# First x by token steps of both streams, the diagonal of reciprocals in two operations, and a first weight slice of 256 columns

## The chip, the cores and the metric

The kernel runs on one core of one Trainium2 chip. The metric is the device time of one execution in microseconds, as the median of several runs. A core has a tensor engine (PE in the profile, its weight loads PEld), a vector engine (DVE), a scalar engine (ACT), GpSimd (POOL), and SyncE (SP), which here issues DMAs only. Each engine works through its own instructions in order and waits for the others by semaphores. DMAs are issued from SP (queue q1, hardware_dynamic) and from GpSimd (queue q0, software_dynamic) and are carried out by 16 DMA engines.

## The reference

A short causal convolution along the sequence, whose taps are a softmax over the kernel positions of each head, and behind it a feed-forward block with a rectified gate:

```python
w = np.exp(weight - weight.max(-1, keepdims=True))
w = w / (w.sum(-1, keepdims=True) + 1e-9)              # [H=8, K=7]
x_pad = zeros(6 rows) + x                               # x: [B=8, S=4096, D=192]
out[b, s, h, g] = sum_k w[h, k] * x_pad[b, s + k, h, g] # head h has 24 of the 192 channels
y = out.reshape(32768, 192)
result = (np.maximum(y @ w_gate, 0) * (y @ w_val)) @ w_out   # 192 -> 1536 -> 192
```

Inputs and output are float32.

## The kernel before, in words

**Streams and units.** The eight sequences are handled as two streams of four (`st` 0 and 1, `NB` = 4 sequences apart). A unit is 1024 tokens of both streams, a window 512 tokens; there are 16 units. A tile of activations holds channel group c (64 of the 192 channels, three groups) of stream 0 on partitions 0 to 63 and of stream 1 on partitions 64 to 127. The gate and value weights (`Wg`, `Wv`) stand on both halves of the partitions, so that the two streams are multiplied side by side.

**Main part.** For each unit, `gate_val` (L528) goes over 12 slices f of 128 hidden columns: 12 matmuls of 512 columns (two weights, three channel groups, two streams), in pairs; ACT takes the gate through a ReLU into `gr` (L552), DVE multiplies it with the value into `hT` (L553). The results stand in PSUM tiles of two banks; the pool `ps` has four buffers that are given out in turn, so f+2 needs the buffers of f. `project` (L636) multiplies `hT` with `Wo` (L570), and ACT and DVE move the result out. For most tokens the convolution is done by ACT, DVE and GpSimd on transposed tiles (the lanes), beside PE's matmuls.

**The start.** For the first windows the convolution runs on PE, as matmuls of x (tokens on partitions) with banded matrices that hold the taps of one head on their diagonals. This is where the change lies. In order of the code:

- SP loads `weight` (L101), then x. The first window of 512 tokens is cut into five token steps `jj`: step 0 has 96 tokens, steps 1 to 4 have 104 each, with 6 rows of the step before. SP brings steps 1 to 4 of stream 0 in float32 into a staging area (`stage`, in the tile `prods`, L122), and step 0 of both streams (L138), whose padding DVE clears first (L137). GpSimd brings steps 1 to 4 of stream 1 with a cast to 16 bits straight into the tile `x_h` (L127).
- GpSimd clears `spaced` (L126), and selects ones on its diagonals (L128); from it DVE makes `same` and `places` by reductions (L238), patterns of ones that spread a coefficient over a band.
- The weights come by columns, in slices `CUTS = [0, 128, 384, 640, 896, 1152, 1536]`, by GpSimd's queue (`load_w`, L167 to L173), onto partitions 0 to 63; a copy (`both_halves`, L175 to L177) brings them to the other half: DVE does slices 0 and 1, GpSimd the later ones. GpSimd issues slices 0 to 2, then the x of the second window (`load_x`, L86), then slices 3 to 5 with copies between.
- Coefficients: DVE the negated maximum (L251), ACT the exponentials into `ex` (L254), DVE their sum and its reciprocal `sm` (L258, L259) and `over` = identity times the reciprocal (L261); PE spreads `over` over the exponentials (L272), DVE makes `diag` (L282), PE makes the bands in PSUM (L292, 14 matmuls). ACT makes `taps` (L304), which SP copies to all partitions in ten small DMAs (L310). `fill_band` moves the bands to SBUF: heads 0 to 3 by DVE, heads 4 to 7 by ACT (L329). The bands of heads 0 to 3 and 4 to 7 stand in two different PSUM tiles, `bps` and `spread`.
- ACT casts the staged steps 1 to 4 of stream 0 (L317), in two parts by channels; DVE casts step 0 (L335).
- `warm_up` (L152 to L155) puts dummy matmuls of ones into the waits of PE: seven ahead of the coefficients (six of 512 columns and one of 256), and one of 512 after each of the two steps that make the bands.
- `first_block` (L387) does the 120 convolution matmuls of the first window (L377), group by group; for group 0 stream 0 comes before stream 1. Each group has its own PSUM tile, and is moved to `xc` by ACT, DVE and ACT (L392). At the start of group 0 DVE copies weight slice 0 to the other half. After the block DVE copies slice 1 (L661), and `gate_val` begins. `second_block` (L394), the same for the next window, stands within the sixth f of the first `gate_val`.

## Time and profile before

| what | value |
|---|---|
| median of 3 runs | 765.98 us (765.98 to 766.01) |
| span of the profiled execution | 764.4 us |
| PE busy | 760.3 us (99%) |
| DVE busy | 705.6 us (92%) |
| ACT busy | 600.9 us (79%) |
| first matmul of the first `gate_val` | at 7.66 us |

The span runs from the first to the last instruction of the profiled execution; the time of a run holds about 1.6 us more than that. In the profile a line of a timeline gives start and length in us, engine, line of the code, operation, output <- inputs, shapes, and in square brackets how long the engine had been idle before and what ended that. A line of the stages gives a stretch of time, then its length, then the busy time of PE, PEld, DVE, ACT and POOL with the number of instructions, the granted clock, the share of the DMA engines and GB/s. A line of the chain gives start, length and what carried the chain in that time. A line of a DMA queue gives packets, MB, and the share of the 16 engines' time.

### The profile page before, as it was taken

To read this page: it belongs to the slowest core of one execution; us is meant where nothing else is said; L and a number is where in the kernel's file an instruction comes from. 1 tells how busy PE (TensorE), PEld (TensorE's weight loads), DVE (VectorE), ACT (ScalarE), POOL (GpSimd) and SP (SyncE) were. 2 spreads that over 40 slices of the span, in tenths; PEclk is the share of its full clock that TensorE was granted. 3 is DMA by queue.
4 is the path that set the end of the run, shared out by engine and by line. 5 is a ranking of instruction groups with operands and counts; after the bars stand their busy time and mean duration, and the time that the engine had idled before them with its cause. 6 is when DMAs were issued, how large, how long until landed. Compare 5 with 4: busy or idle time off the path is not lost.

```text
span 764.4 us, 25103 instructions
## 1 busy us (share of the span) xinstructions
PE 760.3 (99%) x10929; PEld 501.3 (66%) x10929; DVE 705.6 (92%) x763; ACT 600.9 (79%) x735; POOL 378.4 (50%) x244
## 2 busy tenths in 40 slices
PE   9999999999999999999999999999999999999998
PEld 5494674947649476584855848567494674947648
DVE  7998999999999999999999999999999999999891
ACT  6787887878878887887878878787787887876571
POOL 9419448093571926729175390853909347090000
PEclk9999999999999999999999999999999999999999
DMA  9969039290452805528073271722819134220202
GB/s 123 134 102 148 7 96 81 65 111 22 95 67 83 97 23 107 49 85 94 30 112 40 85 94 44 120 16 90 89 44 125 13 97 60 66 48 15 71 1 84
DMA packets 131830, 56.00 MB, mean 73 GB/s; under 512 B 96392, under 2 KB 131720, under 8 KB 131720
## 3 DMA queue, kind: packets, MB, share of 16 engines
q1 hardware_dynamic: 90680, 38.81, 23.9%
q0 software_dynamic: 40896, 15.50, 20.3%
q8 instruction: 85, 1.39, 0.8%
q14 instruction: 25, 0.20, 0.1%
q10 hardware_dynamic: 144, 0.10, 0.0%
HBM read 31.48 MB, written 25.17 MB: 74 GB/s over the span
## 4 chain that ended last, share of the span: by engine, by line
PE 99%; DVE 0%; ACT 0%; issue 0%
PE ps L541 65%; PE ps L570 32%; PE ps L619 1%; PE ps L377 0%; PE ps L154 0%; PE ps L411 0%; DVE band L329 0%; PE ps L272 0%; ACT acc L596 0%; PE ps L292 0%
## 5 line engine op out<-in xcount | busy, mean ns | idle before, releaser
L553 DVE TENSOR_TENSOR hT<-gr,ps 128x1024 f16<-128x1024 f16 (+1 forms) x386 | 469.0, 1216 | 36.6 <-ACT gr L552 9.4
L552 ACT ACTIVATE gr<-ps 128x1024 f16<-128x1024 f32 (+1 forms) x386 | 392.9, 1019 | 101.9 <-PE ps L541 99.7
L491 POOL TENSOR_TENSOR prods<-prods 128x1344 f32<-128x1344 f32 x70 | 212.4, 3034 | 290.0 <-DVE prods L487 286.7
L541 PE MATMUL ps<-xc,Wg 64*128 64x512 f16 x2304 | 311.9, 376 | 0.0
L541 PE MATMUL ps<-xc,Wv 64*128 64x512 f16 x2304 | 311.9, 376 | 0.0
L570 PEld LDWEIGHTS <-hT 64*128 64x128 f16 x5952 | 245.9, 94 | 3.7
L570 PE MATMUL ps<-Wo,hT 64*128 64x192 f16 x5952 | 248.1, 243 | 0.0
L541 PEld LDWEIGHTS <-Wv 64*128 64x128 f16 x2304 | 129.8, 94 | 118.5 <-DVE hT L553 0.3
L541 PEld LDWEIGHTS <-Wg 64*128 64x128 f16 x2304 | 112.3, 94 | 132.8 <-issue 0.2
L515 DVE SCALAR_TENSOR_TENSOR acc<-x_r,tap,acc 128x576 f32<-128x576 f16 x225 | 165.3, 813 | 0.0
L485 ACT ACTIVATE prods<-x_r,tap 128x448 f32<-128x448 f16 x222 | 130.1, 660 | 0.0
L596 ACT COPY out_s<-ps 128x768 f32<-128x768 f32 (+1 forms) x64 | 45.5, 711 | 51.3 <-PE ps L570 40.0
L203 POOL DMA_DIRECT2D x_e<-in_x_dram x58 | 47.0, 823 | 16.6 <-ACT acc L501 12.8
L465 POOL COPY x_p<-x_e 128x960 f16<-128x960 f16 (+1 forms) x58 | 50.3, 906 | 1.2 <-DMA x_e<-in_x_dram 1.1
L491 POOL TENSOR_TENSOR xc<-prods 128x1344 f16<-128x1344 f32 x14 | 42.4, 3029 | 1.1
L515 DVE SCALAR_TENSOR_TENSOR xc<-x_r,tap,acc 128x576 f16<-128x576 f16 x45 | 34.1, 813 | 0.0
L501 ACT ACTIVATE acc<-x_r,tap 128x576 f32<-128x576 f16 x45 | 31.4, 763 | 0.0
L487 DVE TENSOR_SCALAR prods<-x_r,tap 128x448 f32<-128x448 f16 x70 | 26.6, 450 | 0.0
L596 DVE COPY out_s<-ps 128x384 f32<-128x384 f32 (+1 forms) x16 | 8.7, 541 | 11.9 <-PE ps L619 9.4
L619 PE MATMUL ps<-Wo,hT 128*128 128x192 f16 x96 | 8.1, 246 | 0.0
L619 PEld LDWEIGHTS <-hT 128*128 128x128 f16 x96 | 7.9, 98 | 0.2 <-issue 0.2
L154 PE MATMUL ps<-const-bfloat16-1.0 128*128 128x512 bf16 (+1 forms) x9 | 3.9, 572 | 0.8 <-PEq L719 0.8
(54 smaller groups left out, 56.3 us busy)
## 6 DMA issues: line engine op xcount, KB each, us to landing
out_dram<-out_s SPq DMA_DIRECT2D x62, 384.0 KB, 2.7
x_e<-in_x_dram POOLq DMA_DIRECT2D x34, 192.0 KB, 7.4
x_e<-in_x_dram POOLq DMA_DIRECT2D x24, 240.0 KB, 5.6
x_r<-x_p SPq DMA_TRANSPOSE x131, 5.1
Wo<-in_moe_w_out_dram POOLq DMA_DIRECT2D x1, 576.0 KB, 7.3
x_h<-in_x_dram POOLq DMA_DIRECT2D x2, 210.0 KB, 4.8
Wg<-in_moe_w_gate_dram POOLq DMA_DIRECT2D x4, 96.0 KB, 4.1
Wv<-in_moe_w_val_dram POOLq DMA_DIRECT2D x4, 96.0 KB, 4.0
```

Source lines behind the costliest of these rows:

```text
L203: first = nc.gpsimd.dma_start(out=xe[:, j0 + start : j0 + n, st, :, :].rearrange("p j c r -> p j (c r)"), in_=bass.AP(tensor=x.tensor, off ...
L465: nc.gpsimd.tensor_copy(out=xp[:, j0 : j0 + n, :, st, :], in_=xe[:, j0 : j0 + n, st, :, :])
L485: engine.activation(out=out, in_=in_, func=ACTF.Copy, scale=scale)
L487: engine.tensor_scalar(out=out, in0=in_, scalar1=scale, scalar2=None, op0=ALU.mult)
L491: nc.gpsimd.tensor_tensor(out=pr[:, 0] if k < KW - 1 else xc[v + 1][:, :, LDVE:UNIT], in0=pr[:, 0], in1=pr[:, k], op=ALU.add,)
L501: nc.scalar.activation(out=accs[v][:, c, :], in_=shifted(v, c, 0, 0), func=ACTF.Copy, scale=tap[:, c, 0:1],)
L515: nc.vector.scalar_tensor_tensor(out=xc[v][:, c, 0:LDVE] if k == KW - 1 else acc[:, c, :], in0=shifted(v, c, k, 0), scalar=tap[:, c, k : k ...
L541: nc.tensor.matmul(out=pss[i][:, st, :], lhsT=W[64 * st : 64 * st + 64, c, 128 * f : 128 * (f + 1)], rhs=xcb[64 * st : 64 * st + 64, c, WI ...
L552: nc.scalar.activation(out=gr[:, sts], in_=pss[0][:, sts], func=ACTF.Relu)
L553: nc.vector.tensor_tensor(out=h[:, f, sts], in0=gr[:, sts], in1=pss[1][:, sts], op=ALU.mult)
L570: mm = nc.tensor.matmul(out=outs[q], lhsT=h[64 * r : 64 * r + 64, f, st, 128 * q : 128 * (q + 1)], rhs=Wo[64 * r : 64 * r + 64, f, :], sta ...
L596: one(out=dst[:, step * j : step * j + step], in_=src[:, step * j : step * j + step])
```

## The change

- **x by token steps.** SP brings step 1 and step 2 of both streams in a DMA each, then step 0, all staged in float32. GpSimd brings steps 3 and 4, one DMA for each stream. ACT casts steps 1 and 2 (one operation each, both streams), DVE step 0, which now comes after both of DVE's bands.
- **GpSimd's order.** It no longer clears `spaced` (DVE does), and its first work is the DMA of `Wg`'s slice 0, then the selection, then its two x DMAs, then `Wv`'s slice 0, then the rest as before.
- **Slices.** `CUTS` becomes six slices of 256 columns. DVE copies the first 128 columns of slice 0 to the other half before the first block and the other 128 after it, then slice 1.
- **Diagonal.** `ex` has a ninth row: 2 to the 127th off the diagonal and 0 on it, made by DVE from `spaced` ahead of the maximum. `over` is then the sum over all nine rows and its reciprocal: two operations; off the diagonal that is as good as zero. `same` is made between maximum and sum. The sum and reciprocal for the taps are made later, behind `diag`, and the product with them moves from ACT to DVE.
- **Order of the first block.** Group 0 steps 1 and 2, group 1 steps 1 and 2, group 0 step 0, group 0 steps 3 and 4 in another PSUM tile, then the rest of group 1, then group 2. Group 0 is moved to `xc` by ACT in two parts. All four PSUM buffers are taken.
- **Dummies.** One of 512 columns less at the start, and the last one has 256 columns instead of 512.

```diff
--- before.py
+++ after.py
@@ -112,19 +112,38 @@
 
     xts[0] = xpool.tile([128, GSUB, 2, D], F16, name="x_h")
 
-    def body(st):
-        return bass.AP(
-            tensor=x.tensor,
-            offset=x.offset + (NB * st * S + FIRST - PAD) * D,
-            ap=[[D, SUB], [DSUB * D, GSUB - 1], [1, D]],
+    BYSP = 3
+
+    def first_x(jj, rows, tok):
+        nc.sync.dma_start(
+            out=stage(PAD if jj == 0 else 0, rows, 0, 2, jj, 1),
+            in_=bass.AP(
+                tensor=x.tensor,
+                offset=x.offset + tok * D,
+                ap=[[D, rows], [NB * S * D, 2], [1, D]],
+            ),
         )
 
-    nc.sync.dma_start(out=stage(0, SUB, 0, 1, 1, GSUB - 1), in_=body(0))
+    Wg = const.tile([128, NCH, DFF], F16)
+    Wv = const.tile([128, NCH, DFF], F16)
+    Wo = const.tile([128, NFF, D], F16)
+    CUTS = [0, 256, 512, 768, 1024, 1280, DFF]
+
+    def load_w(s, which=3):
+        cols = slice(CUTS[s], CUTS[s + 1])
+        for src, dst in ((moe_w_gate, Wg), (moe_w_val, Wv))[which == 2 : 1 + (which > 1)]:
+            nc.gpsimd.dma_start(
+                out=dst[0:64, :, cols],
+                in_=src.rearrange("(c p) f -> p c f", p=64)[:, :, cols],
+            )
+
+    for jj in range(1, BYSP):
+        first_x(jj, SUB, FIRST - PAD + DSUB * (jj - 1))
     ones = const.tile([128, SUB], FP)
     nc.vector.memset(ones[:], 1.0)
     spaced = const.tile([SUB, KW, SEG + 2 * GAP], FP)
-    nc.gpsimd.memset(spaced[:], 0.0)
-    nc.gpsimd.dma_start(out=xts[0][0:SUB, 1:GSUB, 1, :], in_=body(1))
+    nc.vector.memset(spaced[:], 0.0)
+    load_w(0, 1)
     nc.gpsimd.affine_select(
         out=spaced[:, :, GAP : GAP + SEG],
         in_=ones[0:SUB, 0 : KW * SEG].rearrange("p (k s) -> p k s", k=KW),
@@ -134,13 +153,18 @@
         base=0,
         channel_multiplier=1,
     )
+    for st in range(2):
+        nc.gpsimd.dma_start(
+            out=xts[0][0:SUB, BYSP:GSUB, st, :],
+            in_=bass.AP(
+                tensor=x.tensor,
+                offset=x.offset + (NB * st * S + FIRST - PAD + DSUB * (BYSP - 1)) * D,
+                ap=[[D, SUB], [DSUB * D, GSUB - BYSP], [1, D]],
+            ),
+        )
+    load_w(0, 2)
     nc.vector.memset(stage(0, 32, 0, 2, 0, 1), 0.0)
-    nc.sync.dma_start(
-        out=stage(PAD, FIRST, 0, 2, 0, 1),
-        in_=bass.AP(
-            tensor=x.tensor, offset=x.offset, ap=[[D, FIRST], [NB * S * D, 2], [1, D]]
-        ),
-    )
+    first_x(0, FIRST, 0)
     spare = const.tile([H, 1], FP)
     nc.scalar.activation(spare[:], ones[0:H, 0:1], ACTF.Exp)
 
@@ -155,25 +179,13 @@
                 out=warm[:, n % 2, 0:w], lhsT=busy[:, 0:128], rhs=busy[:, 0:w], start=True, stop=True
             )
 
-    warm_up(512, 512, 512, 512, 512, 512, 256)
-
-
-
-    Wg = const.tile([128, NCH, DFF], F16)
-    Wv = const.tile([128, NCH, DFF], F16)
-    Wo = const.tile([128, NFF, D], F16)
-    CUTS = [0, 128, 384, 640, 896, 1152, DFF]
-
-    def load_w(s, which=3):
-        cols = slice(CUTS[s], CUTS[s + 1])
-        for src, dst in ((moe_w_gate, Wg), (moe_w_val, Wv))[which == 2 : 1 + (which > 1)]:
-            nc.gpsimd.dma_start(
-                out=dst[0:64, :, cols],
-                in_=src.rearrange("(c p) f -> p c f", p=64)[:, :, cols],
-            )
-
-    def both_halves(copy, s, dst):
-        cols = slice(CUTS[s], CUTS[s + 1])
+    warm_up(512, 512, 512, 512, 512, 256)
+
+
+
+    def both_halves(copy, s, dst, half=None):
+        lo, hi = CUTS[s], CUTS[s + 1]
+        cols = slice(lo, hi) if half is None else slice(lo + 128 * half, lo + 128 * half + 128)
         copy(out=dst[64:128, :, cols], in_=dst[0:64, :, cols])
 
     def pool_halves(s):
@@ -218,7 +230,10 @@
                     )
                 yield
 
-    load_w(0)
+    def cast_first(copy, jj):
+        rows = FIRST + PAD if jj == 0 else ROWS0
+        copy(out=xts[0][0:rows, jj, :, :], in_=stage(0, rows, 0, 2, jj, 1))
+
     load_w(1)
     load_w(2)
     load_rest(load_x(1))
@@ -229,8 +244,17 @@
     pool_halves(3)
     load_w(5, 2)
 
-    ex = const.tile([H, KW + 1, SEG], FP)
+    ex = const.tile([H, KW + 2, SEG], FP)
     nc.vector.memset(ex[:], 1e-9)
+    FAR = 2.0**127
+    nc.vector.tensor_scalar(
+        out=ex[:, KW + 1, 0:H],
+        in0=spaced[0:H, 0, GAP : GAP + H],
+        scalar1=-FAR,
+        scalar2=FAR,
+        op0=ALU.mult,
+        op1=ALU.add,
+    )
     some = spaced[:, 0, 0:1]
 
     def summed(out, step, n, at):
@@ -251,22 +275,19 @@
     nc.vector.tensor_reduce(
         out=mx[:], in_=wr[:], axis=mybir.AxisListType.X, op=ALU.max, negate=True
     )
+    same = const.tile([SUB, SEG], FP)
+    summed(same[:], pitch_k, SEG, GAP)
     nc.scalar.activation(
         ex[:, 0:KW, :], wr[:].unsqueeze(2).to_broadcast([H, KW, SEG]), ACTF.Exp, bias=mx[:]
     )
-    sm = const.tile([H, 1], FP)
-    nc.vector.tensor_reduce(out=sm[:], in_=ex[:, :, 0], axis=mybir.AxisListType.X, op=ALU.add)
-    nc.vector.reciprocal(sm[:], sm[:])
     over = const.tile([H, H], FP)
-    nc.vector.tensor_scalar(
+    nc.vector.tensor_reduce(
         out=over[:],
-        in0=spaced[0:H, 0, GAP : GAP + H],
-        scalar1=sm[:],
-        scalar2=None,
-        op0=ALU.mult,
+        in_=ex[:, :, 0:H].rearrange("h k j -> h j k"),
+        axis=mybir.AxisListType.X,
+        op=ALU.add,
     )
-    same = const.tile([SUB, SEG], FP)
-    summed(same[:], pitch_k, SEG, GAP)
+    nc.vector.reciprocal(over[:], over[:])
     summed(places[:, SUB - SEG : SUB - SEG + SEG + KW - 1], pitch_k - 1, SEG + KW - 1, GAP)
     spread = psum.tile([128, 2, 512], FP, name="ps")
     nc.tensor.matmul(
@@ -298,10 +319,17 @@
                 skip_group_check=True,
             )
 
-    warm_up(512)
+    warm_up(256)
 
     taps = const.tile([H, KW], FP)
-    nc.scalar.activation(taps[:], ex[:, 0:KW, 0], ACTF.Copy, scale=sm[:])
+    sm = const.tile([H, 1], FP)
+    nc.vector.tensor_reduce(
+        out=sm[:], in_=ex[:, 0 : KW + 1, 0], axis=mybir.AxisListType.X, op=ALU.add
+    )
+    nc.vector.reciprocal(sm[:], sm[:])
+    nc.vector.tensor_scalar(
+        out=taps[:], in0=ex[:, 0:KW, 0], scalar1=sm[:], scalar2=None, op0=ALU.mult
+    )
     tap = const.tile([128, NCH, KW], FP)
     for h in range(H):
         r = G * h
@@ -313,11 +341,8 @@
             )
             r += n
 
-    for cols in (slice(0, 64), slice(64, D)):
-        nc.scalar.copy(
-            out=xts[0][0:ROWS0, 1:GSUB, 0, cols],
-            in_=stage(0, ROWS0, 0, 1, 1, GSUB - 1)[:, :, cols],
-        )
+    cast_first(nc.scalar.copy, 1)
+    cast_first(nc.scalar.copy, 2)
     bands = {}
 
     def fill_band(a, heads, copy):
@@ -332,10 +357,10 @@
         )
 
     fill_band(0, [0, 1, 2], nc.vector.tensor_copy)
-    nc.vector.tensor_copy(
-        out=xts[0][0 : FIRST + PAD, 0, :, :], in_=stage(0, FIRST + PAD, 0, 2, 0, 1)
-    )
     fill_band(0, [3], nc.vector.tensor_copy)
+    cast_first(nc.vector.tensor_copy, 0)
+    both_halves(nc.vector.tensor_copy, 0, Wg, 0)
+    both_halves(nc.vector.tensor_copy, 0, Wv, 0)
     fill_band(1, [4, 5], nc.scalar.copy)
     fill_band(1, [6, 7], nc.scalar.copy)
 
@@ -349,26 +374,18 @@
     PLACE = {0: (0, 0, 0), 1: (0, 0, 1), 3: (0, 1, 0), 4: (0, 1, 1)}
     PLACE |= {6: (1, 0, 0), 7: (1, 0, 1), 2: (1, 1, 0), 5: (1, 1, 1)}
 
-    def conv_dense(g, c, ps, bank):
+    def conv_dense(g, c, ps, bank, steps):
 
 
         xt = xts[g]
-        if g == 0 and c == 0:
-            xc[0] = xcpool.tile([128, NCH, UNIT], F16, name="xc")
-            both_halves(nc.vector.tensor_copy, 0, Wg)
-            both_halves(nc.vector.tensor_copy, 0, Wv)
         toks = GROUPS[g][1]
         t0 = toks[0]
         ends = toks[1:] + [t0 + WIN]
-        late = (1, 2, 3, 4, 0)
-        both = [(jj, (0, 1)) for jj in late]
-        if g == 0 and c == 0:
-            both = [(jj, (st,)) for st in range(2) for jj in late[0:4]] + both[4:]
-        for jj, sts in both:
+        for jj in steps:
             col, n = toks[jj] - t0, ends[jj] - toks[jj]
             rows = n + PAD
             for second in range(2):
-                for st in sts:
+                for st in range(2):
                     for k2 in range(2):
                         k = 2 * c + k2
                         h0, h1 = 32 * k // G, (32 * k + 31) // G
@@ -385,18 +402,27 @@
                         )
 
     def first_block():
-        for c in range(NCH):
-            ps = psum.tile([128, 2, 512], FP, name="ps")
-            conv_dense(0, c, ps, 0)
-            copy = nc.vector.tensor_copy if c == 1 else nc.scalar.copy
-            copy(out=xc[0][:, c, 0:WIN], in_=ps[:, 0, :])
+        xc[0] = xcpool.tile([128, NCH, UNIT], F16, name="xc")
+        early, late, *rest = [psum.tile([128, 2, 512], FP, name="ps") for _ in range(4)]
+        cut = GROUPS[0][1][BYSP]
+        held, by_pool = (1, 2), range(BYSP, GSUB)
+        conv_dense(0, 0, early, 0, held)
+        conv_dense(0, 1, rest[0], 0, held)
+        conv_dense(0, 0, early, 0, (0,))
+        conv_dense(0, 0, late, 0, by_pool)
+        nc.scalar.copy(out=xc[0][:, 0, 0:cut], in_=early[:, 0, 0:cut])
+        nc.scalar.copy(out=xc[0][:, 0, cut:WIN], in_=late[:, 0, cut:WIN])
+        conv_dense(0, 1, rest[0], 0, (0, *by_pool))
+        nc.vector.tensor_copy(out=xc[0][:, 1, 0:WIN], in_=rest[0][:, 0, :])
+        conv_dense(0, 2, rest[1], 0, (1, 2, 0, *by_pool))
+        nc.scalar.copy(out=xc[0][:, 2, 0:WIN], in_=rest[1][:, 0, :])
 
     def second_block():
         two, one = [psum.tile([128, 2, 512], FP, name="ps") for _ in range(2)]
-        conv_dense(1, 0, two, 0)
-        conv_dense(1, 1, two, 1)
+        conv_dense(1, 0, two, 0, (1, 2, 3, 4, 0))
+        conv_dense(1, 1, two, 1, (1, 2, 3, 4, 0))
         nc.scalar.copy(out=xc[0][:, 0:2, WIN : 2 * WIN], in_=two[:])
-        conv_dense(1, 2, one, 0)
+        conv_dense(1, 2, one, 0, (1, 2, 3, 4, 0))
         nc.vector.tensor_copy(out=xc[0][:, 2, WIN : 2 * WIN], in_=one[:, 0, :])
 
     def conv(g):
@@ -656,6 +682,8 @@
 
 
     first_block()
+    both_halves(nc.vector.tensor_copy, 0, Wg, 1)
+    both_halves(nc.vector.tensor_copy, 0, Wv, 1)
     both_halves(nc.vector.tensor_copy, 1, Wg)
     both_halves(nc.vector.tensor_copy, 1, Wv)
     pool_halves(4)
```

## The prediction, made before the changed kernel ran

> **What bounds the kernel now.** I read the page first, then the busy time by stages, then the chain that ended last in the first 30 us, then each engine's timeline there.
>
> ```profile
> span 764.4 us, 25103 instructions
> PE 760.3 (99%) x10929; PEld 501.3 (66%) x10929; DVE 705.6 (92%) x763; ACT 600.9 (79%) x735; POOL 378.4 (50%) x244
> ```
> ```profile
> 7.65:11.00 3.35, 3.35 (x36) 1.61 (x34) 2.65 (x6) 2.59 (x5) 3.30 (x6) 1.00 1.28 134
> 11.00:24.00 13.00, 13.00 (x228) 6.66 (x228) 11.36 (x11) 10.13 (x11) 12.86 (x18) 1.00 1.10 131
> 24.00:100.00 76.00, 76.00 (x1116) 51.49 (x1114) 71.80 (x77) 62.20 (x81) 35.10 (x25) 1.00 0.58 92
> ```
>
> The second number of a stage is PE's busy time: from 7.65 us on PE has no idle time. The change touches nothing that PE does after that, so it is worth what it moves the start of PE's continuous work, plus any new stall in the first steps of it. The profiled execution has a span of 764.4 us and the runs have a median of 765.98; the 1.6 us between them lie outside the span, and I carry a difference from one to the other unchanged.
>
> ```profile
> 0.85 2.93 PE ps L154 x7
> 3.78 0.47 PE ps L272 x2
> ...
> 5.09 0.52 DVE band L329
> ...
> 5.65 2.08 PE ps L377 x106
> 7.72 6.66 PE ps L541 x60
> 14.38 1.48 PE ps L377 x120
> ```
> ```profile
> 6.18 1.38 PEld L377 LDWEIGHTS <-x_h 110*32 110x32 f16 x104 [0.15 <-DMA x_h<-in_x_dram]
> ...
> 10.96 0.33 PEld L541 LDWEIGHTS <-Wv 64*128 64x128 f16 x6 [0.34 <-DVE hT L553]
> ```
> ```profile
> 7.66 0.39 PE L541 MATMUL ps<-xc,Wg 64*128 64x512 f16 x2
> ```
>
> The start is a chain: coefficients, bands at 5.09, the first block's 120 convolution matmuls from 5.65, the gate from 7.66. In the first block 104 of the 120 had to wait, to 6.18, for the second stream of x, which GpSimd's queue brings; the second block does 120 in 1.48 us, **12.3 ns** each. The last stall is at 10.96, where f=2 waits for DVE's hT: PE is barely held there, but DVE has no more to give. These two, the gate's start and that hT, are where the sum is read.
>
> **The change, part by part.**
>
> ```profile
> 5.12 0.92 ACT L317 CAST x_h<-prods 110x256 f16<-110x256 f32 x2 [1.60 <-DMA prods<-in_x_dram]
> 5.96 0.58 ACT L329 CAST band<-ps 128x224 f16<-128x224 f32 x2
> ...
> 9.00 3.18 ACT L552 ACTIVATE gr<-ps 128x512 f16<-128x512 f32 x5 [0.48 <-PE ps L541]
> ```
>
> *x by token steps.* Before, SP's first x DMA (one stream, steps 1 to 4) has landed at 5.12. After, SP brings steps 1 and 2 of both streams, together the same bytes, then step 0. So I take step 2 as landed at 5.12 and step 1 somewhat before. ACT then has, behind step 2's landing, one cast of 384 elements instead of 768: half of 0.92, 0.46, with both pairs of bands behind it as now. Now it goes from 5.12 to 6.54, 1.42; after, 1.42 - 0.46 = 0.96, so 6.08. PE's order now puts 16 matmuls of channel group 1 (steps 1 and 2) second. They write the PSUM buffer that held half the bands, so they wait for ACT's last band: 6.08, and 6.13 with a handoff. The first 16 matmuls, of group 0, lie ahead of that. Behind the wait stand 120 - 16 = 104 matmuls, as many as stand behind 6.18 now, but now these take 7.66 - 6.18 = 1.48, because 16 of them run for one stream alone; at the second block's pace they take 104 x 12.3 ns = 1.28. The gate starts at 6.13 + 1.28 + about 0.05 = **7.46**, 0.20 earlier.
>
> GpSimd's x, steps 3 and 4, must be there by 6.13 + (16 + 8) x 0.0123 = 6.43; the same queue's x is usable at 6.18 now. That holds if the weights put ahead of it cost under 0.25 us. What decides it:
>
> ```profile
> 0.81 0.33 POOL L126 MEMSET spaced<- 112x280 f32 x1 [0.29 <-POOLq L719]
> 1.42 0.88 POOL L127 DMA_DIRECT2D x_h<-in_x_dram  x1 [0.28 <-issue]
> 2.39 0.36 POOL L128 TENSOR_SCALAR_AFFINE_SELECT spaced<-ones 112x112 f32<-112x112 f32 x1
> 2.67 0.68 POOL L170 DMA_DIRECT2D Wg<-in_moe_w_gate_dram  x1
> ```
> ```profile
> 42.22 0.85 POOL L203 DMA_DIRECT2D x_e<-in_x_dram  x1 [12.75 <-ACT acc L501]
> ```
> ```profile
> q0 software_dynamic: 12, 0.00, 4.2%
> ```
> ```profile
> q1 hardware_dynamic: 45, 0.03, 29.9%
> ```
> ```profile
> q1 hardware_dynamic: 487, 0.36, 104.1%
> ```
>
> The last three rows are the DMA queues in 42.2 to 43.9, 2.2 to 3.0 and 3.0 to 4.1 us. From 2.2 to 3.0 SP's queue (q1) is the only one at work and fills 30% of the engines; from 3.0 to 4.1 it fills them, still alone. GpSimd's x was issued by 2.30 and shows no packet before 4.1. At 42.22 an issue of 0.85, over at 43.07, has its first packets before 43.9, within 0.8 us. So either GpSimd's packets stood behind SP's, or its first issue is slow (1.8 us). After, the first issue is Wg with twice the columns, from 0.8 to 1.1 (the 0.28 of issue time may stay), over at 1.5 to 2.0. With 0.8 us it moves in the 70% that are empty from 2.3 to 3.0: 0.7 x 0.8 = 0.56 us of full engines, about what it needs (192 packets of 1 KB read are 0.2 MB, and q1 moves 0.36 MB in 1.1 us: 0.6 us). With 1.8 us it meets SP's x. I take the former, and keep the latter as rivals. Then GpSimd's x lands at 6.1 to 6.3 and Wv, as long a transfer as both slices now, at about 6.75, as now.
>
> [...]
>
> *Weights and DVE.*
>
> ```profile
> 1.07 0.38 DVE L137 MEMSET prods<- 32x384 f32 x1
> ...
> 2.79 0.15 DVE L258 TENSOR_REDUCE sm<-ex 8x1 f32<-8x8 f32 x1 [0.45 <-ACT ex L254]
> 2.98 0.15 DVE L259 RECIPROCAL sm<-sm 8x1 f32<-8x1 f32 x1
> 3.25 0.22 DVE L261 TENSOR_SCALAR over<-spaced,sm 8x8 f32<-8x8 f32 x1
> 3.39 0.35 DVE L238 TENSOR_REDUCE same<-spaced 112x16 f32<-112x112 f32 x1
> ...
> 5.09 0.51 DVE L329 CAST band<-ps 128x336 f16<-128x336 f32 x1 [0.51 <-PE ps L292]
> 5.67 0.36 DVE L335 CAST x_h<-prods 102x384 f16<-102x384 f32 x1
> ...
> 6.49 0.28 DVE L177 COPY Wg<-Wg 64x384 f16<-64x384 f16 x1 [0.27 <-DMA Wg<-in_moe_w_gate_dram]
> 6.75 0.58 DVE L177 COPY Wv<-Wv 64x384 f16<-64x384 f16 x1
> 7.36 0.69 DVE L392 CAST xc<-ps 128x512 f16<-128x512 f32 x1
> 8.08 0.42 DVE L177 COPY Wg<-Wg 64x768 f16<-64x768 f16 x1
> 8.43 0.53 DVE L177 COPY Wv<-Wv 64x768 f16<-64x768 f16 x1
> 9.62 2.48 DVE L553 TENSOR_TENSOR hT<-gr,ps 128x512 f16<-128x512 f16 x4 [0.67 <-ACT gr L552]
> ```
>
> Ahead of xc (L392) DVE has the same two copies of 384 elements, the second from 6.75. Each takes 0.28 to 0.58, so they are over at 7.03 to 7.33; group 1 is ready 0.30 ahead of the gate (7.36 against 7.66), at 7.16. xc runs from about 7.2 to 7.9. Behind it come two **added** copies (the second half of the 256 columns), 0.56 to 0.86 with their 0.28 to 0.58 each, then slice 1 as now, 8.08 to 8.96, 0.88. DVE is free at 9.35 to 9.75, middle 9.5. The first hT needs ACT's gr as well: 9.62 - 7.66 = 1.96 behind the gate, 9.42. So hT moves from 9.62 to 9.5, the added copies eating the idle 0.67 in front of it, and f=2 with it, from 10.96 to 10.84. Sum: 0.20 won at the gate, 0.08 of it lost to the copies: **-0.12**, with ends -0.2 (ACT decides) and +0.13 (both added copies slow).
>
> *Diagonal.* Now reduction, reciprocal and product go from 2.79 to 3.47, 0.68. After, one reduction over 8 x 9 elements (between 0.15 for 8 and 0.35 for 112; 0.27) and a reciprocal of 8 (0.15 from the row for one; up to 0.22), 0.45 in all, and `same` goes into the wait for the exponential. Against it, the row of large numbers (a product like the 0.22) now stands ahead of the maximum on DVE and waits for GpSimd's selection, whose end I put at 1.95 to 2.45 (the Wg issue, 0.68 to 0.88, then 0.36 and handoffs) against 2.75 now. The maximum moves by 0 to +0.5. The diagonal is ready at 3.25 to 3.75, now 3.47. Either way it is covered: the first 16 matmuls need the bands at 5.9, now 5.60, since the ACT wait stands at 6.13. I count 0, and up to +0.2 if every bound is the bad one. The reciprocal and product for the taps go to DVE between the diagonal and the bands, into the 0.51 of idle time ahead of 5.09: 0.52 there, at most 0.1 over, under the same cover. SP's ten tap DMAs start later, and are read long after this stage. The memset that moves to DVE (280 elements, under the 0.38 for 384) runs beside DMA latency; step 0's DMA waits behind it on SP, up to 0.3 later, and lands at about 5.7 to 6.0 with 0.36 of cast on DVE, wanted at 6.13 + 16 x 0.0123 = 6.33. Just covered.
>
> *Warm-up.* PE loses 768 columns of the dummy matmuls. They hide only in the wait, but the tensor clock opens through them:
>
> ```profile
> 4.18 0.61 PE L154 MATMUL ps<-const-bfloat16-1.0 128*128 128x512 bf16 x1
> ...
> 5.09 0.38 PE L154 MATMUL ps<-const-bfloat16-1.0 128*128 128x512 bf16 x1
> ```
>
> A 512-column matmul takes 0.61 at 4.18 and 0.38 at 5.09: the faster pace came between them, about 4 us behind PE's first matmul. After, the first run of dummies ends 2.93/6.5 = 0.45 earlier, and PE waits that long for the diagonal. I count 0; the other end is rival D. [...]
>
> Slices of 256 columns from the second on are wanted one f later than now; GpSimd's copies of the last shrink. Under a PE that is busy throughout, nothing.
>
> **How it adds up.** 765.98 - 0.12 = 765.86, so **765.9**.
>
> **The rivals.**
>
> A, *more is won*: the group-1 matmuls wait for the first pair of bands alone (half of 0.58 earlier) or x lands earlier. DVE then decides: -0.2 to -0.45, 765.6. For it: bands 4 and 5 are all that they read. Against: the buffer is shared with 6 and 7.
>
> B, *slower: Wg takes turns with SP's x.* Its 0.6 us of transfer stretch step 2's landing by 0.4, to 5.5. ACT, and the gate behind it, go to 7.86, xc to 8.25, hT to 9.85: +0.25, 766.2. It decides from a landing at 5.25, where the 0.12 are gone. For it: a first issue that shows packets only after 1.8 us. Against: q1 alone from 3.0 to 4.1.
>
> C, *Wg stands behind SP's x*: GpSimd's x lands 0.5 later, 6.65; behind it 80 matmuls, 1.0; gate 7.7. Wv lands at 7.25, its copy ends at 7.55 to 7.85, xc at 8.25 to 8.55, hT at 9.7 to 10.3: +0.1 to +0.65, 766.35.
>
> D, *the clock opens late*: conv at half pace (+1.48) and part of the gate: +1.2 to +2, 767.4. For it: less dummy work. Against: PE is still busy most of the time.
>
> E, *the diagonal is no earlier*: covered, the same time as the forecast; it is within it.
>
> **How the numbers follow.** Forecast 0.45, A 0.12, B 0.22, C 0.16, D 0.05. Forecast alone: 765.75 to 766.1. The range takes in A, B and C with their bounds: **765.5 to 766.6**; D is left out, and what my bounds miss at either end, together under 0.2. About 0.2%, 1.5 us, is what a measurement of this kernel can tell from no change; the whole stage that the change touches holds 7.66 us and moves by tenths. Only D reaches past it: slower 0.04, faster 0.01, within 0.95.
>
> **What would show it.** Right: Wg's packets between 2.2 and 3.0 on the software queue; ACT's second cast at about 5.1; conv's second group at about 6.1; gate at 7.45; DVE without idle time from xc to hT, hT at 9.5. Wrong: the second cast at 5.4 or later (B); conv waiting for x_h past 6.4, or xc behind a late Wv copy (C); convolution matmuls at twice 12.3 ns (D); any PE idle time behind 11 us, which I hold for excluded.

## The result, and the profile after

The change makes the kernel slower. After: 768.94 us, median of 6 runs (767.78 to 770.02); before, beside it: 765.98 us (765.92 to 766.41). The ratio is **1.0037 [1.0026, 1.0048]**, +2.96 us; forecast were 765.9 and, at most, 766.6. The runs of the kernel after spread over 2.2 us, those of before over 0.5. The profiled run after took 768.67 us. Times here are medians and ratios compare means; the kernel before has long executions of its own (13 of the 102 beside the experiments took 767.4 to 768.0), which widen every interval.

The page after, and its stages:

```profile
span 766.8 us, 25104 instructions
PE 761.8 (99%) x10928; PEld 503.6 (66%) x10928; DVE 706.4 (92%) x769; ACT 601.3 (78%) x735; POOL 378.0 (49%) x244
```
```profile
0.00:7.65 7.65, 6.04 (x86) 3.49 (x90) 4.31 (x19) 3.80 (x8) 6.43 (x14) 1.00 0.80 129
7.65:11.00 3.35, 3.35 (x82) 1.98 (x72) 2.14 (x6) 0.92 (x3) 3.31 (x6) 1.00 1.28 144
11.00:24.00 13.00, 13.00 (x228) 6.76 (x226) 10.72 (x12) 10.31 (x13) 11.88 (x16) 1.00 0.95 109
```

PE is without idle time from 7.65 us on, as before, and does the same 228 matmuls from 11 to 24 us. So the time, all but 0.4 of it, was lost ahead of 11 us, though in the second row PE is no less busy than it was (matmuls of 24.2 ns count there as busy as those of 12.3, see below). The chain that ended last, to 18 us:

```profile
1.32 0.80 POOL Wg L135
2.13 0.08 POOLq L147 x2
2.20 0.01 issue
2.22 0.36 POOL spaced L147
2.58 0.64 POOL x_h L157
3.22 3.99 DMA x_h<-in_x_dram
7.21 0.04 issue
7.25 1.89 PE ps L394 x60
9.15 7.33 PE ps L567 x53
```

Before, the chain ran through coefficients and bands; now it is GpSimd's second x DMA, third in its queue. The timeline of the same execution shows the rest:

```profile
2.61 0.16 DVE L250 TENSOR_SCALAR ex<-spaced 8x8 f32<-8x8 f32 x1 [0.58 <-POOL spaced L147]
...
3.28 0.26 DVE L284 TENSOR_REDUCE over<-ex 8x8 f32<-8x72 f32 x1 [0.18 <-ACT ex L280]
...
3.58 0.19 DVE L290 RECIPROCAL over<-over 8x8 f32<-8x8 f32 x1
...
3.91 0.51 PE L293 MATMUL ps<-over,ex 8*112 8x8 f32 x2 [0.56 <-DVE over L290]
...
5.36 0.51 ACT L235 CAST x_h<-prods 110x384 f16<-110x384 f32 x1 [1.27 <-DMA prods<-in_x_dram]
...
5.78 0.59 ACT L354 CAST band<-ps 128x224 f16<-128x224 f32 x2
...
7.25 1.89 PE L394 MATMUL ps<-band,x_h 110*32 110x104 f16 x78 [0.19 <-DMA x_h<-in_x_dram]
7.74 0.29 DVE L189 COPY Wv<-Wv 64x384 f16<-64x384 f16 x1 [1.09 <-DMA Wv<-in_moe_w_val_dram]
...
8.33 0.69 DVE L416 CAST xc<-ps 128x512 f16<-128x512 f32 x1 [0.31 <-PE ps L394]
...
9.08 0.61 PE L567 MATMUL ps<-xc,Wg 64*128 64x512 f16 x2
...
10.58 0.38 PE L567 MATMUL ps<-xc,Wg 64*128 64x512 f16 x2
...
11.01 0.81 PE L567 MATMUL ps<-xc,Wg 64*128 64x512 f16 x6
```

Three things stand in it. **x is late**: the 78 matmuls that need it start at 7.25 (before, 104 started at 6.18). **PE runs at half pace**: those 78 take 1.89, 24.2 ns each instead of 12.3, and the gate's first matmuls take 0.61, which becomes 0.38 only at 10.58. The column of the granted clock reads 1.00 throughout; the pace of equal matmuls shows it, and so does the trace's record of the clock, whose entry for the full clock begins at 10.38 here and at 4.78 before; I say that the clock opens there. **The diagonal is late**: DVE's row of large numbers waits for GpSimd's selection to 2.61, and `over` is ready at 3.77 (before 3.47), behind PE's last dummy, which ends at 3.35.

The gate starts at 9.08 instead of 7.66, +1.42: x +1.07, and 9.08 - 7.25 = 1.83 for the 78 matmuls behind it, where 104 took 1.48, +0.35. At the pace of before (1.48 / 104 = 14.2 ns) the 78 would take 1.11. The twelve matmuls of the first f, at half pace to about 10.4, take 1.93 instead of 1.34, +0.59, and f=1 stands at +2.01. So in this execution half pace holds 0.72 (1.83 - 1.11) + 0.59 = 1.31 of it, and the late x, less the 26 matmuls that no longer stand behind it, 1.07 - 0.37 = 0.70. The second block stands at +2.07, and so does ACT's last copy, before and after:

```profile
761.40 0.32 ACT acc L596
```
```profile
763.47 0.32 ACT acc L622
```

The spans end at 764.36 and 766.84, so 0.41 more is lost behind that copy. In the trace SP closes the program with a row of semaphore waits, 0.06 us each; behind the wait for the last output no further one stood before, and seven stand there now. Every kernel of this document that was built from the changed one takes 3.39 to 3.42 us from PE's last matmul to the end of the span, and every one built from the kernel before takes 2.96 to 2.99. So these 0.41 belong to the change, and the smallest part of it that was run (x by steps, below) has them already. 2.01 + 0.06 + 0.41 = 2.48 is the whole difference of the spans; another 0.2 of the profiled run's time lies outside the span.

What the DMA queues moved, before and then after (packets, MB, share of the engines), from 1.5 to 5.1 us and from 5.1 to 6.2:

```profile
q0 software_dynamic: 319, 0.12, 28.0%
q1 hardware_dynamic: 688, 0.49, 50.0%
```
```profile
q0 software_dynamic: 276, 0.12, 30.3%
q1 hardware_dynamic: 696, 0.49, 50.7%
```
```profile
q0 software_dynamic: 640, 0.19, 163.3%
```
```profile
q0 software_dynamic: 330, 0.12, 111.3%
```

By 5.1 us both kernels had moved the same bytes on each queue. But GpSimd's 0.12 MB were x before, and now most of them are `Wg` (192 packets of 512 bytes, 0.10 MB), which landed at 5.14. From 5.1 to 6.2 GpSimd's queue moved 0.12 instead of 0.19 MB. x, 0.17 MB, landed at 7.21 instead of 6.14; `Wv` at 7.72 instead of 6.73.

### The profile page after: what moved, and what is told of

It reads as the page before. It is cut to its first block, busy times and chain, and to the rows that moved or that the text cites. A ratio compares the mean times of both kernels' runs of the same rounds, so it can differ in the third digit from the quotient of the medians.

```text
span 766.8 us, 25104 instructions
## 1 busy us (share of the span) xinstructions
PE 761.8 (99%) x10928; PEld 503.6 (66%) x10928; DVE 706.4 (92%) x769; ACT 601.3 (78%) x735; POOL 378.0 (49%) x244
## 4 chain that ended last, share of the span: by engine, by line
PE 99%; DMA 1%; POOL 0%; issue 0%; ACT 0%; POOLq 0%
PE ps L567 65%; PE ps L596 32%; PE ps L645 1%; DMA x_h<-in_x_dram 1%; PE ps L394 0%; PE ps L437 0%; POOL Wg L135 0%; POOL x_h L157 0%; POOL spaced L147 0%; ACT acc L622 0%; POOLq L147 0%; POOLq L747 0%
## 5 line engine op out<-in xcount | busy, mean ns | idle before, releaser
L579 DVE TENSOR_TENSOR hT<-gr,ps 128x1024 f16<-128x1024 f16 (+1 forms) x386 | 469.1, 1216 | 37.2 <-ACT gr L578 10.4
L394 PE MATMUL ps<-band,x_h 110*32 110x104 f16 (+7 forms) x240 | 4.6, 248 | 0.2 <-DMA x_h<-in_x_dram 0.2
```

Source lines behind the costliest of these rows:

```text
L579: nc.vector.tensor_tensor(out=h[:, f, sts], in0=gr[:, sts], in1=pss[1][:, sts], op=ALU.mult)
```

## The experiments

Theory 1 is the clock: 768 dummy columns less and a later diagonal leave gaps on PE, and the clock opens later, in the two profiles at 10.38 instead of 4.78; the stretch with the open clock is then 757.76 us long instead of 761.17. This step of 3.41 us is what the expectations call a window. Its rivals are the transfers: the order of GpSimd's queue (`Wg` ahead of x) and, formed later and called theory 3, the bytes that have to come through the DMA engines by the first f, whatever their order. Each expectation spells out what it takes for granted. "Dummies of before" are 512 x 6 and 256, and 512 behind the bands; "of after" 512 x 5 and 256, and 256.

### The kernel after, with the dummies of before

```diff
-    warm_up(512, 512, 512, 512, 512, 256)
+    warm_up(512, 512, 512, 512, 512, 512, 256)
...
-    warm_up(256)
+    warm_up(512)
```

> The changed kernel with the dummy matmuls of the kernel before (seven at the start, 512 columns at the end). Theory 1, the clock: the 768 columns less let PE idle from 3.35 to 3.91 us and the clock opens at 10.4 instead of 4.8; with them it opens before the convolution, whose 78 late matmuls then take 1.0 us instead of 1.8 and the first f 1.3 instead of 1.9, so about 1.4 us come back: 767.0 to 767.6, with little spread. Theory 2, the order of the DMAs alone: GpSimd's x still lands at 7.2, PE waits for it anyway, and the time stays 768 to 770 with a late clock.

768.19 us (767.3 to 770.06), 1.0025 [1.0015, 1.0035]. The median is 0.75 lower than that of the change, less than the spread of either (767.78 to 770.02 there), and short of the 767.0 to 767.6 expected. In its profile the clock still opened at 10.21; the dummies did not bring it forward in this execution. x landed at 7.59, with unchanged DMAs: in the four profiles with this order it landed between 6.89 and 7.59.

### The kernel before, with the dummies of after

```diff
-    warm_up(512, 512, 512, 512, 512, 512, 256)
+    warm_up(512, 512, 512, 512, 512, 256)
...
-    warm_up(512)
+    warm_up(256)
```

> The kernel before with only the dummies cut as in the change. Theory 1: the same gap behind 3.35 us makes the clock open late here too; convolution and first f at half pace cost 1 to 2.5 us, 767 to 768.5, with spread. Theory 2: the dummies hide in waits, 765.9 to 766.1.

767.18 us (766.39 to 767.78), 1.0008 [0.9998, 1.0017]. Not one run reached 765.98. The clock opened at 10.03, and with x on time the 120 convolution matmuls took 3.08. So by the medians the dummies alone cost about 1.2 in the kernel before; by the means the interval still holds 1.

### The kernel after, x ahead of the weights on GpSimd

```diff
-    load_w(0, 1)
     nc.gpsimd.affine_select(
...
-    load_w(0, 2)
+    load_w(0)
```

> The changed kernel with GpSimd's two x DMAs ahead of Wg's slice 0 (order: selection, x, x, Wg, Wv), dummies as in the change. Theory 2: x of steps 3 and 4 lands at 6.2 to 6.4 instead of 7.2, the gate starts about 0.9 earlier, 767.9 or less. Theory 1: the clock is late as well, and half of the win is lost to matmuls at half pace, 768 to 768.6.

The second run has the dummies of before as well:

> Both together: x first and the dummies of before. If the two causes add up, clock at 4.8 and x at 6.2 to 6.4, the gate starts at 7.4 and the time is 765.7 to 766.0. If one of them hides the other, it is no better than the better one of the two.

With the dummies of after 768.41 (5 runs), 1.0031 [1.0018, 1.0044], the clock open at 12.95 in its profile; with those of before (the second) 767.99, 1.0022 [1.0012, 1.0031]. In the second x landed at 6.58, the clock opened at 5.94 and the gate started at 7.71, as good as before. Yet 765.7 to 766.0 had been expected: the loss had moved, and the 0.41 at the end stayed.

```profile
7.71 0.59 PE L566 MATMUL ps<-xc,Wg 64*128 64x512 f16 x2
...
8.31 0.69 DVE L415 CAST xc<-ps 128x512 f16<-128x512 f32 x1
...
9.06 0.39 PE L566 MATMUL ps<-xc,Wg 64*128 64x512 f16 x2 [0.33 <-DVE xc L415]
```

`Wv` came at 7.97; its copy stands on DVE ahead of xc, so xc was cast at 8.31, though its matmuls were done, and PE waited to 9.06. In this order `Wv` is late, in the order of the change x.

### One size: the slices

```diff
-    CUTS = [0, 128, 384, 640, 896, 1152, DFF]
+    CUTS = [0, 256, 512, 768, 1024, 1280, DFF]
```

> The kernel before with the column cuts of the change alone (first slice 256 wide, copied in one piece). Theory 3, the queue's budget: all that the first gate needs comes through DMA engines that are full from 3 us on, so the 0.2 MB more that lie ahead of the gate bring Wv's slice 0 about 0.5 later, to 7.25; its copy and xc behind it end at 8.4 instead of 8.05 and the gate stalls by about 0.4: 766.3 to 766.6. Theory 1 (only the clock matters): 765.9 to 766.1.

This edit in the kernel before: 766.31 (766.30 to 766.43), 1.0002 [0.9992, 1.0012], the narrowest spread of all runs.

```profile
6.99 0.53 DVE L177 COPY Wv<-Wv 64x768 f16<-64x768 f16 x1
7.40 0.39 PE L541 MATMUL ps<-xc,Wg 64*128 64x512 f16 x2
7.54 0.69 DVE L392 CAST xc<-ps 128x512 f16<-128x512 f32 x1
```

The gate was ready at 7.40, xc only at 8.23, f=1 began 0.15 later than before, and the second block 0.24 later. The interval holds 1, but all ten runs lie above 22 of the 28 of the kernel before beside them. The next run undoes it in the kernel with x first and the dummies of before:

```diff
-    CUTS = [0, 256, 512, 768, 1024, 1280, DFF]
+    CUTS = [0, 128, 384, 640, 896, 1152, DFF]
...
-    both_halves(nc.vector.tensor_copy, 0, Wg, 1)
-    both_halves(nc.vector.tensor_copy, 0, Wv, 1)
```

> The changed kernel with x ahead of the weights, the dummies of before, and the narrow first slice of before (128 columns, no second half to copy). In the run before this with the wide slice, the clock opened at 5.9 and the gate began at 7.7, but it stalled because Wv's slice landed at 7.97: median 768.0. Theory 3: with half the bytes Wv lands at about 7.3, the stall of 0.7 goes, and executions with an early clock take 766.0 to 766.4. Theory 1: the stall is covered by the late clock, and the median stays at 767.5 to 768.

767.0, 1.0013 [1.0004, 1.0022], between what the two theories expected, f=1 at 9.12 instead of 9.92. So by the medians the wide slice costs 0.3 where transfers are early and **1.0** where they are late.

### The diagonal

The ninth row, the two operations and the taps of the change, in the kernel before:

```diff
+    nc.vector.tensor_scalar(
+        out=ex[:, KW + 1, 0:H],
...
-    nc.vector.tensor_scalar(
+    nc.vector.tensor_reduce(
         out=over[:],
...
+    nc.vector.reciprocal(over[:], over[:])
...
-    nc.scalar.activation(taps[:], ex[:, 0:KW, 0], ACTF.Copy, scale=sm[:])
+    nc.vector.tensor_scalar(
+        out=taps[:], in0=ex[:, 0:KW, 0], scalar1=sm[:], scalar2=None, op0=ALU.mult
+    )
```

> The kernel before with the diagonal and the taps of the change alone. The row of large numbers stands ahead of the maximum on DVE and waits for GpSimd's selection, which ends at 2.75 here, so the exponential moves from 2.37 to about 3.0 and the bands from 5.09 to about 5.5, by less than the operations saved. Theory 3: x of stream 1 lands at 6.14 anyway, 16 matmuls of the first block move behind it, +0.1 to +0.3. Theory 1: the wait of PE ahead of the diagonal grows by 0.5 as in the change, and the clock opens late in more of the executions: 767 to 768 in those.

767.1 (766.1 to 768.39), 1.0009 [0.9998, 1.0019].

```profile
2.78 0.16 DVE L235 TENSOR_SCALAR ex<-spaced 8x8 f32<-8x8 f32 x1 [1.05 <-POOL spaced L128]
...
3.75 0.19 DVE L275 RECIPROCAL over<-over 8x8 f32<-8x8 f32 x1
...
6.24 2.77 PE L390 MATMUL ps<-band,x_h 110*32 110x104 f16 x120
```

`over` was ready at 3.95, 0.48 later than before, because the maximum waited behind the row of large numbers. In this execution the clock opened at 8.54 and the 120 matmuls took 2.77, 23 ns each. Other runs of the same kernel reached 766.1. They have no trace; that the clock opened early in them, and the later diagonal was covered, is likely and not shown.

The reverse, the diagonal and the taps of before in the kernel after:

```diff
-    nc.vector.tensor_reduce(
+    nc.vector.tensor_scalar(
         out=over[:],
...
-    nc.vector.reciprocal(over[:], over[:])
```

> The changed kernel with the diagonal and the taps of before. In the change DVE's maximum moved from 2.19 to 2.69, behind the selection, and the diagonal was ready at 3.77 instead of 3.47; PE waited 0.56 for it behind the dummies. Theory 1, the clock: with the old diagonal that wait is about 0.15, the clock opens by 7 us in more executions, and the median falls by 0.5 to 1.2, to 767.8 to 768.4, with the lowest executions where they are (767.3 to 767.8). Theory 3, the queue's budget alone: x still lands at 7.2, 768.9.

769.48, 1.0038 [1.0026, 1.0051], not better. PE's spread of the coefficients came at 3.61 instead of 3.91, but x at 7.45, and the clock opened at 13.43. Theory 1 alone expected a gain; it missed (5 runs).

### PE filled through the waits of the first block

```diff
         conv_dense(0, 1, rest[0], 0, held)
+        fill(512)
         conv_dense(0, 0, early, 0, (0,))
+        fill(512, 512)
```

> The changed kernel with the dummies of before and three more of 512 columns in the two waits of the first block (behind group 1's first 16 matmuls, and ahead of the matmuls that wait for GpSimd's x). Nothing of the DMAs is changed. Theory 1: PE has no wait over 0.2 us from the start of the convolution on, the clock opens by about 8.2 instead of 10.2, and the median falls from 768.2 to 767.3 to 767.8. Theory 3: x lands at 7.2 to 7.6 and Wv at 8, and the time stays at 768.0 to 768.4.

With the dummies of before and three more (`fill` is a dummy matmul): 767.61 (7 runs, 767.43 to 769.65), 1.0023 [1.0011, 1.0036]. The median is 1.33 lower than that of the change, again within the spread of both. In its profiled run (767.57) the clock opened at 3.72, the matmuls ran at full pace, and the gate still started at 8.66. x had landed at 6.89; what the last 80 matmuls then waited for were the dummies themselves:

```profile
6.89 0.27 PE L394 MATMUL ps<-band,x_h 102*32 102x96 f16 x8
7.09 0.61 PE L411 MATMUL ps<-const-bfloat16-1.0 128*128 128x512 bf16 x2
...
7.63 1.09 PE L394 MATMUL ps<-band,x_h 110*32 110x104 f16 x80
```

f=1 stands at 9.97, +0.97, with no matmul at half pace from 3.72 on; 0.54 of that are these two dummies. Without them some 0.4 would be left of the late transfers, as an estimate. The rest of this run's loss is the 0.41 at the end and what lies outside the span. That the clock holds 1.31 of the change's loss is read from the profile above; the medians agree with it, and do not show it by themselves.

### The transfers alone, in the kernel before

The gate's slice of 128 columns ahead of GpSimd's x:

```diff
+    load_w(0, 1)
     nc.gpsimd.dma_start(out=xts[0][0:SUB, 1:GSUB, 1, :], in_=body(1))
...
-    load_w(0)
+    load_w(0, 2)
```

> The kernel before with Wg's narrow slice 0 alone moved ahead of x in GpSimd's queue. Theory 3: the issue costs 0.65 to 0.8 and its transfer 0.3; x of stream 1 lands 0.5 to 0.8 later than 6.1, the gate starts by as much later, less what the earlier Wg gives back (nothing): lowest executions 766.4 to 766.8. Theory 1: PE's wait for x grows too, and more executions lose a window: 767.5 to 768.5 in those. If the order in GpSimd's queue is free, 765.9 to 766.1.

766.76, 1.0013 [1.0004, 1.0022].

```profile
7.01 1.54 PE L378 MATMUL ps<-band,x_h 110*32 110x104 f16 x104 [0.57 <-DMA x_h<-in_x_dram]
```

`Wg` put ahead, 0.05 MB, moved x from 6.14 to 6.97. x's own issue on GpSimd began 0.73 later too, at 2.15 instead of 1.42. The same 104 matmuls stand behind it; the gate starts at 8.48, +0.82, and the time is up by 0.78. The clock opened at 5.88, ahead of them all. Whether x paid for the transfer of `Wg` or for its issue is not separated: from 4.9 to 5.1, while x was under way, GpSimd's packets, the only ones, took 28% of the engines' time.

The clearing of `spaced` on DVE:

```diff
-    nc.gpsimd.memset(spaced[:], 0.0)
+    nc.vector.memset(spaced[:], 0.0)
```

> The kernel before with only the clearing of spaced moved from GpSimd to DVE. GpSimd's first DMA was issued at 1.42 behind the clearing, and at 1.32 in the change without it. Theory 3: x of stream 1 is issued and lands 0.1 earlier, and the gate with it: 765.85 to 765.95 in the lowest executions. Otherwise no difference, 765.9 to 766.0. Theory 1 expects no more late executions than before.

765.98, 0.9999 [0.999, 1.0008]. No effect.

x by steps, the new first block and the clearing on DVE; dummies, slices and diagonal of before, weights behind x:

```diff
-    nc.sync.dma_start(out=stage(0, SUB, 0, 1, 1, GSUB - 1), in_=body(0))
+    for jj in range(1, BYSP):
+        first_x(jj, SUB, FIRST - PAD + DSUB * (jj - 1))
...
-    nc.gpsimd.dma_start(out=xts[0][0:SUB, 1:GSUB, 1, :], in_=body(1))
+    for st in range(2):
+        nc.gpsimd.dma_start(
+            out=xts[0][0:SUB, BYSP:GSUB, st, :],
```

> The changed kernel's x by steps, first block and clearing on DVE, with the dummies, the narrow first slice, the diagonal and the taps of before, and both weights behind GpSimd's x. Against the run with the new diagonal (lowest 766.65, median 767.0) it tells what the diagonal costs. Theory 3: step 0 lands last of SP's three, at 6.2, and GpSimd's x at 6.6; the gate starts at 7.7, no earlier than before: lowest 766.0 to 766.6. Theory 1: the clock opens as in the kernel before, so nine of ten executions are within 0.3 of the lowest, and the median falls to 766.1 to 766.7.

767.14, 1.0014 [1.0005, 1.0022]. From 5.1 to 6.2 us the queues, and then PE:

```profile
q0 software_dynamic: 446, 0.13, 110.5%
```
```profile
6.80 1.22 PE L380 MATMUL ps<-band,x_h 102*32 102x96 f16 x88 [0.47 <-DVE x_h L234]
```

With no weights ahead and the clock open at 5.55, this part alone costs 1.1, more than either theory expected. Step 0, now third on SP and beside GpSimd's x, landed at 6.37 (before 5.65), and the matmuls waited for it to 6.80: the gate starts at 7.96, +0.30. `Wv` landed at 7.82 (before 6.73), and xc stands behind its copy: f=1 starts at 9.77, +0.77. These and the 0.41 at the end make up the 1.17 by which the spans differ. GpSimd's queue moved 0.13 MB where it moved 0.19; and its issues are later, since the selection now stands ahead of two x DMAs: `Wv` was issued at 3.87 instead of 3.34, half of its 1.09.

### More dummies, and none, in the kernel before

```diff
-    warm_up(512)
+    warm_up(512, 512)
```

> The kernel before with one more dummy of 512 columns behind the bands (two instead of one). Theory 1: the executions of the kernel before at 767.4 to 767.95 (13 of 81 so far) are those in which the clock opens a window late; with more dummy work they become rarer, while the others cost nothing where the clock is open and up to 0.3 where it isn't: 766.0 to 766.3. If the late executions have another cause, their share stays at about one in six.

766.03, 1.0003 [0.9994, 1.0011]: nothing. Whether the clock opens late less often, 11 runs can't tell (one took 768.06). And none at all:

```diff
-    warm_up(512, 512, 512, 512, 512, 512, 256)
...
-    warm_up(512)
...
-    warm_up(512)
```

> The kernel before with no dummy at all. [...] That gives the price of the whole clock effect beside unchanged DMAs: if the change's 2.96 were the clock alone, the two medians would be alike. Theory 3: the dummies hide in waits and only the DMAs count: 766.0.

767.08, 1.0015 [1.0006, 1.0024].

```profile
5.80 2.86 PE L374 MATMUL ps<-band,x_h 110*32 110x104 f16 x120 [0.22 <-DVE band L326]
...
8.59 0.39 PE L538 MATMUL ps<-xc,Wg 64*128 64x512 f16 x2
```

All 120 matmuls at half pace (23.8 ns), the clock open at 8.25, just ahead of the gate: +0.93 at the gate, +1.1 in the time. The two medians are not alike: the change takes 768.94, so its 2.96 is not the clock alone. Beside the transfers of before the clock is worth about 1.1 in the median; in the profiled run with fewer dummies, where it opened at 10.03, the loss was 1.7 (767.66).

### The parts one by one

| kernel | time, us | step |
|---|---|---|
| before | 765.98 | |
| x by steps, first block, clearing | 767.14 | +1.16 |
| and the diagonal | 767.0 | -0.14 |
| and the wide slices | 767.99 | +0.99 |
| and `Wg` ahead of x | 768.19 | +0.20 |
| and fewer dummies: after | 768.94 | +0.75 |

Only the first and the third step stand clear of the spread of their runs (eight of ten runs without the wide slices, and none with them, lie below 767.3); the last three rows' kernels overlap (767.54 to 768.26, 767.3 to 770.06, 767.78 to 770.02). The first holds the 0.41 at the end. No version beat the kernel before.

## Why the prediction was wrong, step by step

**"It moves in the 70% that are empty from 2.3 to 3.0": wrong, and the first step to fail.** The wait behind an issue came out as forecast (0.8, and 0.76 measured: `Wg`'s issue ended at 2.12, first packet at 2.88), with some luck: in the three other profiles with this order it was 1.13 to 1.43. But the issue began at 1.32 and not at 0.8 to 1.1: it had only 0.1 us of the gap, which from 2.3 to 3.0 is 0.7 us long and was reckoned as 0.8. And the gap was gone: SP's first DMA, now half as large, ran in it. The queues after from 2.2 to 3.0 us, where SP moved 0.03 MB before:

```profile
q1 hardware_dynamic: 185, 0.14, 65.7%
q0 software_dynamic: 4, 0.00, 6.7%
```


**"Then GpSimd's x lands at 6.1 to 6.3": 7.21. "Wv at about 6.75, as now": 7.72.** Both followed from `Wg` costing nothing. Two things were left out. In the kernel before, the engines were full (SP's packets took 104% of their time from 3.0 to 4.1, GpSimd's 163% from 5.1 to 6.2), so a transfer put ahead may push back what is behind. And x's own issue moved: 1.42 before, 2.50 and 3.22 after, behind `Wg`'s issue of 0.80, the selection and each other; that is no term of the sum. Together they cost x 0.83 with 0.05 MB ahead in the kernel before, and 1.07 with 0.10 MB here, both against 6.14, the latest landing of x in six profiles with the DMAs of before (5.67 to 6.14). No run tells the two apart. It is what rival C foretold (the matmuls wait for x past 6.4), at twice its 0.5, though not by its mechanism: `Wg` did not stand behind SP's x, it shared the engines with it.

**"Step 2 landed at 5.12": 5.34**, with ACT's cast at 5.36. The two queues do share the engines, as rival B had it: from 3.0 to 4.1 both stand in the trace, with about half of the engines' time each:

```profile
q0 software_dynamic: 133, 0.07, 52.7%
q1 hardware_dynamic: 159, 0.11, 49.0%
```

I had read SP's lone row of before as evidence against B. It was none: GpSimd had shown no packet at all in that time. Together they moved 0.18 MB in that stretch, where SP alone had moved 0.36 before; why the two move less than the one is not shown. But the step cost only 0.24 and held nothing up: ACT's last band was over at 6.37, well ahead of x.

**"The diagonal is covered, 0" and "I count 0" for the warm-up: wrong together.** The diagonal came at 3.77, just past the stated 3.25 to 3.75. It was covered as far as the bands go. What was not covered was PE's own idle time: dummies over at 3.35, next matmul at 3.91, then the wait for x. I saw the clock as a thing that opens "through the dummies" and gave rival D 0.05, because "PE is still busy most of the time". In the change's profile half pace holds 1.31; the runs of the kernel before without or with fewer dummies show +1.1 and +1.2 in the median, D's "+1.2 to +2" at its lower end. No trace of before shows that lower end; these two medians stand in its place.

**C and D as separate cases: wrong.** The change has both at once: PE waits for x, and the matmuls behind the wait run at half pace. Each alone cost about 0.8 (`Wg` ahead) to 1.2 (fewer dummies) in the kernel before. Whether one brings on the other is open: where the clock had opened before the wait for x (at 5.55 to 5.94 in three profiles) it stayed open, and where it hadn't it opened at 10.2 to 13.4; but it was also late, at 8.25 to 10.03, in three profiles whose x was on time.

**The end of the program: no term of the sum.** The prediction held the change to be "worth what it moves the start of PE's continuous work, plus any new stall in the first steps of it". Behind PE's last matmul 0.41 came on top.

**Right:** ACT's chain was 0.29 off (6.37 against 6.08); the added copies took 0.27 to 0.35 and held up nothing; behind f=2 PE showed no further loss.

**Open:** why GpSimd's queue, alone or nearly so from 5.1 to 6.2, moved 0.12 to 0.15 MB in four kernels with x by steps or `Wg` ahead, and 0.19 before. What decides, from run to run, when the clock opens. And what orders SP's waits at the end.

## What to carry to other kernels

Where the DMA engines are full at the start (here 104% from 3.0 to 4.1 and 163% from 5.1 to 6.2), treat an order of transfers as a budget: read the bytes that each queue has moved by each deadline, and charge what goes ahead, its issue and its bytes, to what comes behind (0.83 in the kernel before, for one issue and 0.05 MB). A stretch of the engines that is empty in the old profile may be filled by a changed DMA on another queue: SP's took 29.9% from 2.2 to 3.0 before and 65.7% after. Idle time of PE that is "covered" was not free here: with no dummies, or fewer, the kernel before took 1.1 and 1.2 more in the median, and in their profiles the clock opened at 8.25 and 10.03 instead of 4.78. Look for equal matmuls at two paces (24.2 and 12.3 ns), and count the late transfer and the half pace together. And compare the ends of the two profiles as well as their starts (0.41 here).

## What the runs showed of the hardware

- The lengths of the stretch with the open clock were 761.17, 757.76 and 754.35 us in the fifteen traces that hold the record: always 3.41 us apart. They began at 3.72 to 13.43 us.
- What a late clock cost was read from what ran at half pace until then: all 120 matmuls at 23.8 instead of 12.3 ns in the run without dummies (open at 8.25), +0.93 at the gate; with part of the first f as well, in the profiled run with fewer dummies (open at 10.03), 1.6 at f=1.
- GpSimd's first DMA began at 1.32 to 1.38 with nothing ahead of it, at most 0.10 earlier than behind a memset of 0.33. Its packets came 0.76 to 1.86 us behind the end of the issue. One issue took 0.63 to 0.91 us.
